# Attention ahead of two mixtures: row maxima scaled on ScalarE, the last batch turned in fp32 inside the loop, first weights of the second mixture split among the attention's units

## The chip, the cores and the metric

The kernel runs on one core of a Trainium2 chip. A core has TensorE (PE; its weight loads are shown as PEld), VectorE (DVE), ScalarE (ACT), GpSimd (POOL) and SyncE (SP), which here only issues DMAs. The metric is device microseconds of one execution. Lower is better.

## The reference

Three stages follow one another: a sparse attention, a mixture of eight experts in which each token goes to one expert, and a second mixture in which every token goes through all eight.

```python
# attention: B, H, S, D = 4, 8, 576, 64
scores = q @ k.T / 8                      # per batch and head
# heads 0-3: 0 <= i - j < 32;  heads 4-7: 0 <= i - j < 128 and (i - j) % 4 == 0
attn = softmax(where(mask, scores, -1e9));  x = attn @ v      # -> x [2304, 512]

# first mixture: N, D, E, F = 2304, 512, 8, 1024, capacity 288
logits = x @ w_gate
# pairs (token, expert) in falling order of logits; a token takes the first expert with room
out[mask_e] = relu(x[mask_e] @ w1[e]) @ w2[e]

# second mixture
P = exp(x @ w_gate - max); eight times: rows, then columns scaled to sums (Sinkhorn)
out = sum_e P[:, e] * (relu(x @ w1[e]) @ w2[e])
```

## The kernel before

The order of the instructions on each engine is written out by hand: the program emits them in the order in which each engine is to run them, and each engine and each DMA queue works through its own list in that order, waiting where an operand isn't ready.

**Attention** (`attention`, line 107). Queries go in 24 blocks of 96 (4 batches of 6). The dilated heads have their tokens reordered on the host so that both kinds of heads look at a band of 128 keys. A *unit* (`UNITS`, 25 of them, numbered 0 to 24) is one block of the plain heads (kind 0) with the next block of the dilated ones (kind 1); the first and the last unit are halves. The loop over `n` is a pipeline: step n takes the scores and row maxima of unit n, the transposes of unit n-1 and the products with v of unit n-2. Its order per step is: `scores(n)` on TensorE (line 167 adds the masks, line 174 is q times k); `row_max(n)` on VectorE (line 180 the maximum of 8 rows of 128, line 181 its product with -0.125, from a small tile `negc`); `p_trans(n-1)` on TensorE (line 197), copied to SBUF on VectorE (line 204); `exps(n)`, eight activations on ScalarE with the scaled maximum as bias (line 189); `pv(n-2)` on TensorE (line 215) with, from unit 13 on, products of one ready chunk of 128 tokens with the gate (`logits`, line 280), and on VectorE the reciprocal of the sums and the normalised block `xt` (lines 219 to 221) and the copy of the gate product (line 282); last `x_out(n-3)`, which splits `xt` into two fp16 halves `xo`: the high half copied by ScalarE (line 232), the low half by a subtraction on GpSimd (line 234; for the last two units on VectorE), and stores them to `xd` in HBM through SP's queue (line 237). `xo` has two buffers.

The gate needs x transposed. For batches 0 to 2 a transposing DMA brings chunks back from `xd` (line 262). Blocks of the last batch keep their `xo` in SBUF, and `x_turn` transposes its halves on TensorE (line 250, fp16, eight per unit) and copies them with ScalarE into `xl` (line 254). This is done for seven units behind the steps 24, 25, 26 and 27 (`TURN`). The last five chunks of gate products follow (line 280), and their copy ends the attention (line 335).

All q and k of batches 1 to 3 and v of batch 1 are sent for ahead of the loop (lines 121, 125).

**First mixture** (`Moe.stage1`, line 1146). `Router.phase(0)` finds the first expert and its tokens: VectorE compares all logits with thresholds (line 476), TensorE counts (line 480), VectorE picks a digit (lines 482 to 490), six times over. Between these steps `warm` runs filler products on TensorE (line 643), 5 or 1 at a time, and a generator `w0 = self.weights(("b", 0), ...)` loads six of eight pieces (128 x 1024, fp32, 512 KB) of the second mixture's first expert and splits them: high half on ScalarE (line 679), low half on VectorE (line 680). Then 16 filler products, and the first expert's own work: its weights are gathered by GpSimd (line 700) and split by the same two lines, its tokens gathered (line 709), transposed (line 744) and multiplied (lines 731, 768). The remaining two pieces of `("b", 0)` follow in its course. The other experts' routing is interleaved with the products from there on; the second mixture's first expert is computed block by block (lines 731 and 812), the other seven in `stage2`.

Of the kernel before, what the change touches and what calls it, by code (L numbers as in the profile page):

```python
# [23 lines left out]
QB = 96  # L24
# [59 lines left out]
TURN = {NU - 1: (NU - 7, NU - 6), NU: (NU - 5, NU - 4), NU + 2: (NU - 2, NU - 1)}  # L84
# [22 lines left out]
def attention(tc, q, k, v, masks, wg, ident, xd, L, zero):  # L107

    nc = tc.nc
    with ExitStack() as ctx:  # L110
# [8 lines left out]
        def load_qk(nm, b, kind):  # L119
            x = raw[nm, b, kind] = one.tile([128, 2, S], F32, name="raw%s%d%d" % (nm, kind, b))  # L120
            nc.sync.dma_start(x, src[nm][b, :, 2 * kind:2 * kind + 2])
# [13 lines left out]
        negc = one.tile([QB, 2, 4], F32)  # L135
        nc.gpsimd.memset(negc, -SC)
# [40 lines left out]
        def row_max(u):  # L177
            p, gs = SS[u], part(u, 4)
            nm = wk.tile([QB, 2, 4], F32, name="nm")
            nc.vector.tensor_reduce(nm[:, :, gs], p[:, :, gs], axis=AX.X, op=OP.max)  # L180
            nc.vector.tensor_mul(nm[:, :, gs], nm[:, :, gs], negc[:, :, gs])
            PP[u] = nm

        def exps(u):
            p, nm, gs = SS.pop(u), PP[u], part(u, 4)
            e = wk.tile([QB, 2, 4, 128], F32, name="e")
            for s in range(2):
                for g in range(gs.start, gs.stop):
                    nc.scalar.activation(e[:, s, g, :], p[:, s, g, :], AF.Exp, bias=nm[:, s, g:g + 1], scale=SC)
            PP[u] = e  # L190
# [15 lines left out]
        def pv(u, extra):  # L206
            t = PT.pop(u)
            tag, bufs = ("ps_v", 1) if u + 1 < NU else ("ps_s", 2)
            p = ps.tile([128, 2, 512], F32, name=tag, bufs=bufs)
            pp = p[:QB, :, :4 * (D + 1)].rearrange("p k (h d) -> p k h d", h=4)  # L210
            hs, ks = part(u, H), part(u, 2)
            for h in range(hs.start, hs.stop):
                o = pp[:, h // 4, h % 4, :]
                b, j = UNITS[u][h // 4]
                nc.tensor.matmul(o, t[:, h % 2, h // 2, :], VR[b, h // 4][:, j, h % 4, :], start=True, stop=True)  # L215
            fin = [logits(p[:, 0, 480 + E * n:480 + E * (n + 1)], c) for n, c in enumerate(extra)]
            rc = wk.tile([QB, 2, 4, 1], F32, name="rc")
            xt = wk.tile([QB, 2, 4, D], F32, name="xt")
            nc.vector.tensor_scalar(rc[:, ks], pp[:, ks, :, D:], 1e-9 / SX, None, op0=OP.add)
            nc.vector.reciprocal(rc[:, ks], rc[:, ks])  # L220
            nc.vector.tensor_mul(xt[:, ks], pp[:, ks, :, :D], rc[:, ks].to_broadcast([QB, ks.stop - ks.start, 4, D]))
            XT[u] = xt
            for f in fin:
                f()

        def x_out(u):
            xt, ks = XT.pop(u), part(u, 2)
            if u in XO:
                xo = XO[u]
            else:  # L230
                xo = wk.tile([QB, 2, 2, 4, D], F16, name="xo")
# [10 lines left out]
        def x_turn(*units):  # L242

            for u in units:
                p = ps.tile([128, 2, 512], F32, name="ps_s").bitcast(F16)[:, :, :4 * QB].rearrange(
                    "p k (c q) -> p k c q", c=4)
                ks = part(u, 2) if u > (B - 1) * NJ else slice(1, 2)
                for kind in range(ks.start, ks.stop):
                    for c in range(4):
                        nc.tensor.transpose(p[:, kind, c, :], XO[u][:, kind, c // 2, 2 * (c % 2):2 * (c % 2) + 2, :],  # L250
                                            idh)
                for kind in range(ks.start, ks.stop):
                    for o, n, tok, st in tokens_of(QB * UNITS[u][kind][1], QB, kind):
                        nc.scalar.activation(xl[kind][:, :, tok:tok + st * (n - 1) + 1:st], p[:, kind, :, o:o + n],
                                             AF.Copy)

        XB, XO = {}, {}
# [8 lines left out]
        def left(c, a, x):  # L266

            t0 = 128 * c - S * (B - 1)
            if x == 0:
                return XB[c][:, a, :]  # L270
            return xl[a // 4][:, a % 4, max(t0, 0):t0 + 128]

        def logits(p, c):
            cut = S * (B - 1) - 128 * c
            for x, rows in ((0, slice(0, min(cut, 128))), (1, slice(max(cut, 0), 128))):
                n = 0
                for kt in range(4 if rows.start < rows.stop else 0):
                    hi = kt if kt < 2 else kt + 2
                    for a, w in ((hi, wgh), (hi, wgl), (hi + 2, wgh)):
                        nc.tensor.matmul(p[rows], left(c, a, x), w[:, kt, :], start=(n == 0), stop=(n == 11))  # L280
                        n += 1
            return lambda: nc.vector.tensor_copy(L[:, c, :], p)
# [5 lines left out]
        for b in range(1, B if True else 2):  # L288
            for kind in (1, 0):
                for nm in "kq":  # L290
                    load_qk(nm, b, kind)
            if b == 1:
                for kind in (1, 0):
                    load_v(b, kind)
        nc.scalar.activation(wgh, wgf, AF.Copy, scale=SG)
        nc.vector.scalar_tensor_tensor(wgl, wgf, SG, wgh, op0=OP.mult, op1=OP.subtract)
        xl = [one.tile([128, 4, S], F16, name="xl%d" % kind) for kind in range(2)]
        for n in range(NJ + 1):
            XO[(B - 1) * NJ + n] = one.tile([QB, 2, 2, 4, D], F16, name="xo%d" % n)
        first = S * (B - 1) // 128  # L300
        for n in range(NU + 3):
# [5 lines left out]
            if n < NU:  # L307
                exps(n)
            if n in FILL:
                warm(FILL[n])  # L310
            if n == NU + 1:
                x_turn(NU - 3)
            if 2 <= n <= NU + 1:
                pv(n - 2, [loaded.pop(0)[1] for _ in range(1 if n < NU else 2) if loaded and loaded[0][0] <= n])
# [3 lines left out]
            if n >= 3:  # L318
                x_out(n - 3)
# [9 lines left out]
            x_turn(*TURN.get(n, ()))  # L329
        p = ps.tile([128, 2, 512], F32, name="ps_v", bufs=1)  # L330
        rest = [i for _, i in loaded] + list(range(first, NT))
# [61 lines left out]
class Router:  # L393
# [39 lines left out]
    def start(self, ctx):  # L433
        self.wk = ctx.enter_context(self.tc.tile_pool(name="r_wk", bufs=2))
# [169 lines left out]
class Moe:  # L604
    def __init__(self, ctx, tc, router, xd, ident, w1a, w2a, wg2, w1b, w2b, out, ps, zero):
        nc = self.nc = tc.nc
        self.tc, self.r, self.xd, self.out, self.ps = tc, router, xd, out, ps
# [3 lines left out]
        self.big, self.raw, self.sm = pool("m_big", 1), pool("m_raw", 4), pool("m_s", 1)  # L611
# [3 lines left out]
        self.acc = self.big.tile([128, NT, DM], F32, name="acc")  # L615
# [6 lines left out]
        self.W, self.balanced, self.scattered = {}, False, []  # L622
        self.wb = [[self.big.tile([128, 4, 7, 256], F16, name="w%d%s" % (n, c)) for c in "hl"] for n in (1, 2)]
# [11 lines left out]

    def psum(self):
        return self.ps.tile([128, 512], F32, name="mm", bufs=6)
# [7 lines left out]
    def weights(self, key, letter, fetch, some=slice(None)):  # L645
# [9 lines left out]
        todo = todo[some]  # L655
        live, tiles = [], {lay: t for (k, lay), t in self.W.items() if k == key}
# [13 lines left out]
        for n in range(len(todo)):  # L670
            (lay, k, per, m), r = live.pop(0)
            if lay not in tiles:
                if letter == "a":
                    tiles[lay] = [self.wp.tile([128, (KT, FT)[lay], m], F16, name="w%d%s" % (lay, c)) for c in "hl"]
                else:
                    tiles[lay] = self.wflat[lay]
                self.W[key, lay] = tiles[lay]
# [468 lines left out]
    def stage1(self, ctx):  # L1146

        pool = lambda n, b: ctx.enter_context(self.tc.tile_pool(name=n, bufs=b))
# [4 lines left out]
        self.wp = pool("m_w", 1)  # L1153
# [8 lines left out]
        for _ in w0:  # L1162
            pass
# [6 lines left out]
        def fetched(ph):  # L1170
            w = self.weights(("a", ph), "b", self.fetch_gather(ph))
# [5 lines left out]
        first = itertools.chain(fetched(0), self.weights(("b", 0), "a", self.fetch_static(0), slice(6, None)))  # L1177

        self.ready = self.direct(1)
        def main():  # L1180
# [10 lines left out]
            for ph in range(E):  # L1191
# [8 lines left out]
                for i, ns in enumerate(self.moe1(ph)):  # L1200
                    if ph + 1 == E and i in (16, 40, 44, 52, 56):
                        next(self.ready)
                    if ph == 0 and i % 6 == 1 and ws[0] is first:
                        pump(ph, FT + 4)
                        if ws[1] == FT + 4:
# [20 lines left out]
        self.warm(16)  # L1226
# [65 lines left out]
def tile_kernel(ctx, tc, q, k, v, wg, w1a, w2a, wg2, w1b, w2b, masks, ident, rtab, thr, out):  # L1292
    nc = tc.nc
    with tc.manual_schedule():
# [5 lines left out]
        attention(tc, q, k, v, masks, wg, ident, xd, L, router.zero)  # L1300
        ps = ctx.enter_context(tc.tile_pool(name="ps", bufs=2, space=bass.MemoryType.PSUM))
        router.ps = ps
        moe = Moe(ctx, tc, router, xd, ident, w1a, w2a, wg2, w1b, w2b, out, ps, router.zero)
        with ExitStack() as stage:
            moe.stage1(stage)
# [21 lines left out]
```

## Time and profile before

| | |
|---|---|
| three runs, us | 1835.52, 1838.80, 1842.16 (median 1838.80) |
| profiled execution, us | 1833.92 |
| its span, first to last instruction, us | 1832.1 |
| busy in the span | PE 96%, PEld 71%, DVE 75%, ACT 46%, POOL 12% |
| mean granted TensorE clock | 0.979 of full speed |

The profile is of one execution. The span leaves out 1.8 us around the instructions. Attention ends at 128.2 us, the first expert's routing at 161.8 us. Names like `xo` or `w0l` are the program's tiles; `out<-in` gives what an instruction writes and reads, with shapes as partitions x elements. In brackets stands how long the engine had been idle before the instruction and what ended that. Matmul ends are modelled, so a TensorE that looks busy may be waiting a little.

### The profile page before, as it was taken

The numbers are of one execution on the slowest core, as the hardware profiler recorded it, in microseconds if no ns is written. First come the engines' busy times: TensorE is split into PE (matmuls) and PEld (weight loads), VectorE is DVE, ScalarE is ACT, GpSimd is POOL, SyncE is SP. The second block draws the span as 40 slices with busy tenths as digits, with TensorE's granted clock in tenths as the row PEclk, the third lists the DMA queues.
The fourth block names the chain that finished last, engine by engine and source line by source line (L and its number), as shares of the span: only waits on it lengthen the run. The fifth ranks groups of instructions, "written<-read, shape, count | busy, mean of one in ns | idle before, by whom it ended". The sixth has DMA issues, their size and how long they took to land.

```text
span 1832.1 us, 35300 instructions
## 1 busy us (share of the span) xinstructions
PE 1752.7 (96%) x14518; PEld 1297.8 (71%) x14518; DVE 1371.9 (75%) x2625; ACT 839.1 (46%) x1502; POOL 227.4 (12%) x284
## 2 busy tenths in 40 slices
PE   8986899999999889999999999999999999999998
PEld 6873666666677647766777777777777777777776
DVE  5877776686744767877887888788878878887656
ACT  4662333333344344564444555444555444554333
POOL 1224222233221000000000000000000000000111
PEclk8988899999999999999999999999999999999999
DMA  8554323343242314433244432444352353433120
GB/s 304 148 138 138 110 83 95 109 119 104 88 142 83 122 47 156 147 131 146 112 167 164 184 125 105 171 156 152 136 195 93 127 213 140 163 122 141 55 96 35
DMA packets 106161, 241.19 MB, mean 132 GB/s; under 512 B 46704, under 2 KB 70512, under 8 KB 99088
## 3 DMA queue, kind: packets, MB, share of 16 engines
q1 hardware_dynamic: 84736, 151.34, 23.9%
q0 software_dynamic: 20592, 87.53, 13.4%
q8 instruction: 113, 1.85, 0.4%
q14 instruction: 48, 0.39, 0.1%
q10 hardware_dynamic: 672, 0.08, 0.0%
HBM read 173.83 MB, written 61.73 MB: 129 GB/s over the span
## 4 chain that ended last, share of the span: by engine, by line
PE 70%; DVE 11%; issue 10%; ACT 4%; DMA 3%; POOL 1%; SPq 0%; POOLq 0%; ACTq 0%; DVEq 0%
PE mm L995 26%; PE mm L1033 22%; PE mm L731 8%; PE mm L812 5%; PE mm L768 2%; PE ps_v L215 1%; PE r L480 1%; PE ps_p L197 1%; DVE hl L952 1%; PE ps_s L174 1%; POOL out_dram L1047 1%; DVE w1l L680 1%; DMA wgf<-in_wg_dram 1%; DMA rawk<-in_k_dram 1%; DVE G L552 1%
## 5 line engine op out<-in xcount | busy, mean ns | idle before, releaser
L995 PE MATMUL mm<-xb,w1h 128*128 128x384 f16 x2352 | 574.6, 327 | 5.3 <-DVE mm L966 4.9
L1033 PE MATMUL mm<-w2h,hh 128*128 128x256 f16 x1764 | 480.8, 273 | 8.5 <-DVE t L1059 4.4
L1033 PE MATMUL mm<-w2h,hl 128*128 128x256 f16 x1764 | 480.8, 273 | 0.0
L1033 PE MATMUL mm<-w2l,hh 128*128 128x256 f16 x1764 | 480.8, 273 | 0.0
L995 PE MATMUL mm<-xb,w1l 128*128 128x384 f16 x1176 | 383.9, 326 | 0.0
L1033 PEld LDWEIGHTS <-hh 128*128 128x128 f16 x3528 | 345.2, 98 | 52.6 <-issue 10.6
L995 PEld LDWEIGHTS <-w1h 128*128 128x128 f16 x2352 | 230.4, 98 | 159.5 <-issue 11.6
L1033 PEld LDWEIGHTS <-hl 128*128 128x128 f16 x1764 | 172.6, 98 | 20.0
L952 DVE TENSOR_TENSOR hl<-r,hh 128x1536 f16<-128x1536 f32 x84 | 147.5, 1756 | 41.2 <-ACT hh L951 41.2
L995 PEld LDWEIGHTS <-w1l 128*128 128x128 f16 x1176 | 115.2, 98 | 76.5 <-issue 0.7
L947 ACT ACTIVATE r<-mm 128x384 f32<-128x384 f32 x252 | 119.0, 481 | 98.3 <-PE mm L995 98.3
L951 ACT ACTIVATE hh<-r 128x1536 f16<-128x1536 f32 x84 | 124.6, 1483 | 46.4 <-DVE r L976 44.4
L913 POOL DMA_DIRECT2D ws<-raw x48 | 26.0, 541 | 941.1 <-ACT raw L864 673.6
L958 ACT ACTIVATE mm<-mm 128x384 f32<-128x384 f32 x84 | 40.3, 479 | 180.8 <-PE mm L995 180.8
L952 DVE TENSOR_TENSOR hl<-S,hh 128x1152 f16<-128x1152 f32 x84 | 113.6, 1352 | 0.0
L731 PE MATMUL mm<-xt,w1h 128*128 128x288 f16 x512 | 97.2, 289 | 1.4 <-ACT xt L745 1.4
L1043 DVE SCALAR_TENSOR_TENSOR acc<-t,P,acc 128x512 f32<-128x512 f32 x126 | 94.8, 752 | 4.5
L951 ACT ACTIVATE hh<-S 128x1152 f16<-128x1152 f32 x84 | 96.4, 1147 | 0.0
L864 ACT ACTIVATE raw<-raw 128x1024 f16<-128x1024 f32 x48 | 50.6, 1055 | 96.6 <-DVE raw L849 47.7
L734 ACT ACTIVATE w1h<-mm 128x288 f16<-128x288 f32 (+1 forms) x120 | 47.1, 397 | 102.6 <-PE mm L731 100.5
L735 DVE SCALAR_TENSOR_TENSOR w1l<-mm,w1h 128x288 f16<-128x288 f32 (+1 forms) x120 | 50.7, 435 | 55.1 <-ACT w1h L734 54.5
L731 PE MATMUL mm<-x2l,w0h 128*128 128x256 f16 x288 | 81.1, 282 | 6.8 <-DVE x2l L773 6.8
(258 smaller groups left out, 2972.1 us busy)
## 6 DMA issues: line engine op xcount, KB each, us to landing
xb<-xw SPq DMA_DIRECT2D x30, 1344.0 KB, 5.6
ws<-raw POOLq DMA_DIRECT2D x48, 448.0 KB, 2.7
ws<-r POOLq DMA_DIRECT2D x48, 448.0 KB, 3.0
raw<-in_w2b_dram SPq DMA_DIRECT2D x32, 512.0 KB, 9.4
raw<-in_w1b_dram SPq DMA_DIRECT2D x56, 256.0 KB, 6.3
w1h<-ws SPq DMA_DIRECT2D x6, 1792.0 KB, 7.5
w1l<-ws SPq DMA_DIRECT2D x6, 1792.0 KB
w2h<-ws SPq DMA_DIRECT2D x6, 1792.0 KB
```

Source lines behind the costliest of these rows:

```text
L731: nc.tensor.matmul(p, a[:, k, 128 * f:128 * (f + 1)], rhs(k, b), start=(k == 0 and i == 0), stop=(k == KT - 1 and i == 2))
L734: nc.scalar.activation(h[0][:, f, :n], p, AF.Relu)
L735: nc.vector.scalar_tensor_tensor(h[1][:, f, :n], p, 0.0, h[0][:, f, :n], op0=OP.max, op1=OP.subtract)
L812: nc.tensor.matmul(p, a[:, f, c], b[:, f, :], start=(f == 0 and n == 0), stop=(f == FT - 1 and n == 2))
L864: self.nc.scalar.activation(hi[:, k], x, AF.Copy, scale=sw)
L947: nc.scalar.activation(o, p, AF.Relu, scale=SH)
L951: yield nc.scalar.activation(hq[0][:, i, k], x, AF.Copy)
L952: yield V.tensor_sub(hq[1][:, i, k], x, hq[0][:, i, k])
L958: nc.scalar.activation(Q[i], P[i], AF.Copy)
L995: nc.tensor.matmul(p, w[u][:, 2 * j + i // 2, k, 128 * (i % 2):128 * (i % 2 + 1)], x[:, v, r, j], start=(q in (1, 5) and j == 0 and n == 0 ...
L1033: nc.tensor.matmul(p, h[u][:, i, a, 128 * t:128 * (t + 1)], w[v][:, i, b, :], start=(q in (1, 7) and i == 0 and j == 0), stop=(q in (2, 3) ...
L1043: V.scalar_tensor_tensor(self.acc[:, r, :], x, self.P[:, r, e:e + 1], self.acc[:, r, :], op0=OP.mult, op1=OP.add)
```

## The change

1. The product of the row maxima with -0.125 goes from VectorE to ScalarE (`row_max`). In step n the copy and subtraction of `x_out(n-3)` are emitted between the two halves of the exponentials, where they stood at the end of the step. `xo` gets four buffers, `xt` three.
2. The last batch is turned from `xt`, in fp32: `x_turn(u, p)` makes two transposes per kind into a free part of the tile of `pv`, then the high halves with ScalarE and the low halves with VectorE. Units 18 to 22 are turned in steps 21 to 25, ahead of that step's `pv`; units 23 and 24 behind the loop, ahead of their `x_out`. `xl` is laid out by half.
3. q and k of batches 2 and 3 are sent for in steps 6, 7, 12 and 13; only batch 1 is sent for ahead of the loop.
4. All eight pieces of the second mixture's first weights are loaded and split in the attention by a generator `first_weights`, called once in each step from 4 on: two steps with two loads each, then half a piece a step, with VectorE's half one step behind ScalarE's. The splits in `stage1` and in the first expert's products are gone.
5. For this, `Moe` is constructed ahead of the attention: its load of the identity (SP) and the cast of it (GpSimd) now stand ahead of the attention's loads. The pools of stage 1 lie on the other side of SBUF, and the large tiles are made behind the attention.
6. Filler products: 3 in place of 5 in the first routing, 6 in place of 16 behind it. More chunks of gate products are done in the steps, fewer behind them.

```diff
         def row_max(u):
...
-            nc.vector.tensor_mul(nm[:, :, gs], nm[:, :, gs], negc[:, :, gs])
+            nc.scalar.activation(nm[:, :, gs], nm[:, :, gs], AF.Copy, scale=-SC)
...
-        def pv(u, extra):
+        def pv(u, extra, turn=None):
...
+            if turn is not None:
+                x_turn(turn, p)
             for h in range(hs.start, hs.stop):
...
+            xo = wk.tile([QB, 2, 2, 4, D], F16, name="xo", bufs=4)
...
+        def x_turn(u, p):
+
+            p = p[:, :, 264:264 + 2 * QB].rearrange("p k (c q) -> p k c q", c=2)
+            ks = part(u, 2) if u > (B - 1) * NJ else slice(1, 2)
+            for kind in range(ks.start, ks.stop):
+                for c in range(2):
+                    nc.tensor.transpose(p[:, kind, c, :], XT[u][:, kind, 2 * c:2 * c + 2, :], idf[:QB, :QB])
+            parts = [(xl[kind][:, x, :, tok:tok + st * (n - 1) + 1:st], p[:, kind, :, o:o + n], x)
+                     for x in range(2) for kind in range(ks.start, ks.stop)
+                     for o, n, tok, st in tokens_of(QB * UNITS[u][kind][1], QB, kind)]
+            hi = [o for o, _, x in parts if x == 0]
+            for n, (o, i, x) in enumerate(parts):
+                if x == 0:
+                    nc.scalar.activation(o, i, AF.Copy)
+                else:
+                    nc.vector.tensor_sub(o, i, hi[n - len(hi)])
...
-        for n in range(NU + 3):
+        for n in range(NU + 2):
...
-            if n < NU:
-                exps(n)
+            ex = exps(n) if n < NU else iter(())
+            next(ex, None)
+            if 3 <= n <= NU:
+                x_out(n - 3)
+            for _ in ex:
+                pass
...
+            if n >= 2:
+                pv(n - 2, [loaded.pop(0)[1] for _ in range(1 if n < NU else 3) if loaded and loaded[0][0] <= n],
+                   n - 3 if NU - 4 <= n <= NU else None)
+            if 4 <= n:
+                next(side, None)
...
+            b, c = divmod(n - NJ, NJ)
+            if 0 <= b < B - 2 and c < 2:
+                for nm in "kq":
+                    load_qk(nm, b + 2, 1 - c)
...
+        x_turn(NU - 2, ps.tile([128, 2, 512], F32, name="ps_s"))
+        x_turn(NU - 1, ps.tile([128, 2, 512], F32, name="ps_p", bufs=1))
+        x_out(NU - 2)
+        x_out(NU - 1)
...
+    def first_weights(self, ctx):
...
+        for n, (lay, k, per, m) in enumerate(todo):
+            r = live.pop(0).rearrange("p k f -> p (k f)")
+            hi, lo = (t[:, k:k + per, :].rearrange("p k f -> p (k f)") for t in self.W[("b", 0), lay])
+            for c in (slice(0, 512), slice(512, 1024)):
+                nc.scalar.activation(hi[:, c], r[:, c], AF.Copy, scale=(SW1, SW2)[lay])
+                yield
+                nc.vector.scalar_tensor_tensor(lo[:, c], r[:, c], (SW1, SW2)[lay], hi[:, c], op0=OP.mult,
+                                               op1=OP.subtract)
+                if c.stop == 1024 and n + 4 < len(todo):
+                    load(n + 4)
...
-        w0 = self.weights(("b", 0), "a", self.fetch_static(0), slice(6))
-        next(w0)
         for i, need in enumerate(self.r.phase(0)):
-            self.warm(1 if need < 2000 else 5)
-            if i % 2 and i < 14:
-                next(w0, None)
+            self.warm(1 if need < 2000 else 3)
...
-        first = itertools.chain(fetched(0), self.weights(("b", 0), "a", self.fetch_static(0), slice(6, None)))
+        first = fetched(0)
...
-        self.warm(16)
+        self.warm(6)
...
-        attention(tc, q, k, v, masks, wg, ident, xd, L, router.zero)
...
+        moe = Moe(ctx, tc, router, xd, ident, w1a, w2a, wg2, w1b, w2b, out, router.zero)
         with ExitStack() as stage:
+            attention(tc, q, k, v, masks, wg, ident, xd, L, router.zero, moe.first_weights(stage))
+            moe.after_attention(ctx)
             moe.stage1(stage)
```

## Rows read from the trace of the kernel before

**Rows 1.** Chain of waits, two stretches: start us, us, what, instructions.

```profile
54.79 0.44 PE ps_s L167 x4
58.43 0.44 PE ps_s L167 x4
...
106.51 0.28 PE ps_v L280 x12
```

**Rows 2.** Timeline of VectorE (DVE), one unit: start us, duration us, instruction.

```profile
72.22 1.21 DVE L180 TENSOR_REDUCE nm<-ps_s 96x8 f32<-96x1024 f32 x1
73.46 0.83 DVE L181 TENSOR_TENSOR nm<-nm,negc 96x8 f32<-96x8 f32 x1
74.22 0.94 DVE L204 COPY pt<-ps_p 128x768 f32<-128x768 f32 x1
75.09 0.15 DVE L219 TENSOR_SCALAR rc<-ps_v 96x8 f32<-96x8 f32 x1
...
75.57 0.69 DVE L221 TENSOR_TENSOR xt<-ps_v,rc 96x512 f32<-96x512 f32 x1
...
76.25 1.21 DVE L180 TENSOR_REDUCE nm<-ps_s 96x8 f32<-96x1024 f32 x1
```

**Rows 3.** Timeline of GpSimd (POOL), the same unit.

```profile
73.12 1.15 POOL L234 TENSOR_TENSOR xo<-xt,xo 96x512 f16<-96x512 f32 x1 [2.88 <-ACT xo L232]
```

**Rows 4.** Timeline of ScalarE (ACT), the same unit.

```profile
72.39 0.65 ACT L232 ACTIVATE xo<-xt 96x512 f16<-96x512 f32 x1
74.41 2.15 ACT L189 ACTIVATE e<-ps_s,nm 96x128 f32<-96x128 f32 x8 [1.37 <-DVE nm L181]
```

**Rows 5.** Timeline of VectorE, the attention from unit 4 to its end.

```profile
27.13 1.22 DVE L180 TENSOR_REDUCE nm<-ps_s 96x8 f32<-96x1024 f32 x1 [0.32 <-PE ps_s L174]
...
53.95 0.16 DVE L181 TENSOR_TENSOR nm<-nm,negc 96x8 f32<-96x8 f32 x1
...
100.47 1.21 DVE L180 TENSOR_REDUCE nm<-ps_s 96x8 f32<-96x1024 f32 x1
...
112.57 0.68 DVE L180 TENSOR_REDUCE nm<-ps_s 96x4 f32<-96x512 f32 x1
...
128.00 0.20 DVE L335 COPY L<-ps_v 128x40 f32<-128x40 f32 x1 [3.30 <-PE ps_v L280]
```

**Rows 6.** Timeline of ScalarE, the first 42 us.

```profile
14.96 0.23 ACT L295 ACTIVATE wgh<-wgf 128x32 f16<-128x32 f32 x1 [11.98 <-DMA wgf<-in_wg_dram]
...
39.47 0.63 ACT L232 ACTIVATE xo<-xt 96x512 f16<-96x512 f32 x1 [4.62 <-DMA xd<-xo]
```

**Rows 7.** Stretch, its us, busy time by engine, then PEclk, DMA share, GB/s.

```profile
36.00:50.00 14.00, 11.63 (x85) 10.05 (x84) 7.38 (x13) 6.35 (x21) 3.46 (x3) 0.64 0.26 83
```

**Rows 8.** Line 254, 125 to 127 us: duration ns min/median/max, starts, form.

```profile
L254 ACT ACTIVATE xl<-ps_s x3: 491/585/1018, 125.1 to 126.3; 128x384 f16<-128x384 f16 x3
```

**Rows 9.** Timeline of TensorE (PE) at the start, first product.

```profile
12.13 0.38 PE L167 MATMUL ps_s<-mk,idb 96*96 96x256 bf16 x2 [4.60 <-DMA mk<-in_masks_dram]
```

**Rows 10.** Timeline of GpSimd at the start, the load of the masks.

```profile
2.64 0.55 POOL L148 DMA_DIRECT2D mk<-in_masks_dram  x1
```

**Rows 11.** Timeline of VectorE at the start, first use of the router's table.

```profile
7.02 0.23 DVE L425 CAST tri<-rtab 128x128 f16<-128x128 f32 x1 [5.61 <-DMA rtab<-in_rtab_dram]
```

**Rows 12.** Timeline of VectorE, routing of the first expert and after it.

```profile
132.39 0.27 DVE L482 TENSOR_SCALAR ok<-r,rem 8x64 f16<-8x64 f32 x1 [0.77 <-PE r L480]
132.94 0.23 DVE L488 TENSOR_SCALAR pen<-r 128x64 f32<-128x64 f32 x1 [0.27 <-PE r L485]
...
139.03 0.24 DVE L482 TENSOR_SCALAR ok<-r,rem 8x32 f16<-8x32 f32 x1 [0.47 <-PE r L480]
...
140.33 0.17 DVE L488 TENSOR_SCALAR pen<-r 128x32 f32<-128x32 f32 x1
...
176.27 1.23 DVE L680 SCALAR_TENSOR_TENSOR w2l<-raw,w2h 128x1024 f16<-128x1024 f32 x1 [2.73 <-ACT w2h L679]
```

**Rows 13.** Line 680 alone in a stretch: us, DVE busy (count), PEclk, DMA.

```profile
128.20:162.00 33.80, 7.26 (x6) 0.80 0.40 126
```

More of the change, by code (lines that the diff above doesn't have):

```diff
@@ L104, in lay_v, with attention @@
     return out
-def attention(tc, q, k, v, masks, wg, ident, xd, L, zero):
+def attention(tc, q, k, v, masks, wg, ident, xd, L, zero, side):
     nc = tc.nc
@@ L226, in x_out @@
         def x_out(u):
[L227 to L231, printed above, removed]
+            xt, ks = XT[u], part(u, 2)
+            xo = wk.tile([QB, 2, 2, 4, D], F16, name="xo", bufs=4)
             nc.scalar.activation(xo[:, ks, 0], xt[:, ks], AF.Copy)
@@ L240, in x_out @@
                         xo[p0:p0 + n, kind].rearrange("q a h d -> q (a h d)"))
[L242 to L257, printed above, removed]
+        def x_turn(u, p):
[13 more added lines that the diff above has]
+                    nc.vector.tensor_sub(o, i, hi[n - len(hi)])
+        XB = {}
         def x_load(c, c1):
@@ L328, in attention @@
                 x_load(first, first + 1)
-            x_turn(*TURN.get(n, ()))
+            if n == NU:
+                loaded += [(n, i) for i in (first, first + 1)]
+        x_turn(NU - 2, ps.tile([128, 2, 512], F32, name="ps_s"))
+        x_turn(NU - 1, ps.tile([128, 2, 512], F32, name="ps_p", bufs=1))
+        x_out(NU - 2)
+        x_out(NU - 1)
         p = ps.tile([128, 2, 512], F32, name="ps_v", bufs=1)
-        rest = [i for _, i in loaded] + list(range(first, NT))
+        rest = [i for _, i in loaded] + list(range(first + 2, NT))
         o = p[:, 0, :E * len(rest)].rearrange("p (n e) -> p n e", e=E)
@@ L604, with __init__ @@
 class Moe:
-    def __init__(self, ctx, tc, router, xd, ident, w1a, w2a, wg2, w1b, w2b, out, ps, zero):
+    def __init__(self, ctx, tc, router, xd, ident, w1a, w2a, wg2, w1b, w2b, out, zero):
         nc = self.nc = tc.nc
-        self.tc, self.r, self.xd, self.out, self.ps = tc, router, xd, out, ps
+        self.tc, self.r, self.xd, self.out = tc, router, xd, out
         self.w = {"a": (w1a, w2a), "b": (w1b, w2b)}
@@ L643, in warm, with weights @@
             self.nc.tensor.matmul(p, self.zero[:, :128], self.zero, start=True, stop=True)
-    def weights(self, key, letter, fetch, some=slice(None)):
+    def weights(self, key, fetch):
         nc = self.nc
@@ L654, in weights @@
                 todo.append((lay, k, per, m))
-        todo = todo[some]
-        live, tiles = [], {lay: t for (k, lay), t in self.W.items() if k == key}
+        live, tiles = [], {}
         def load(it):
@@ L672, in weights @@
             if lay not in tiles:
[L673 to L677, printed above, removed]
+                self.W[key, lay] = tiles[lay] = self.wflat[lay]
             hi, lo = (t[:, k:k + per, :] for t in tiles[lay])
```

92 lines of the change are left out of this document (46 added, 46 removed).

## Prediction

> **What bounds the kernel now.** I read the chain of waits first, then the timelines of the engines, unit by unit. The change touches only the attention (to 128.2 us) and the start of the first mixture, so the question is what sets the end there. In the early units the chain is TensorE without a gap: one unit takes 58.43 - 54.79 = 3.64 us [rows 1]. From about 58 us a unit takes 76.25 - 72.22 = 4.03 us, with gate products or without, and VectorE has no gap in it [rows 2]: the maximum 1.24 us to the next start, the multiplication with the negative scale 0.76, the copy of the turned exponentials 0.87, and reciprocal, product and gate copy 1.16. The multiplication has 8 elements a row and lasts 0.83 us where GpSimd's subtraction runs beside it, but 0.16 us alone [rows 2, 5]; it ends at 74.29, with GpSimd's instruction, at 73.12 + 1.15 = 74.27 [rows 3]. It waits for GpSimd, and the exponentials start 0.12 us behind it [rows 4]. One stall stands out: at 39.47 ScalarE had waited 4.62 us for the store of an earlier xo [rows 6], and TensorE's granted clock averages 0.64 around it [rows 7]. Behind the attention, the first expert's routing is a chain through VectorE, and six weight splits of line 680 (7.26 us) stand in it [rows 13].
>
> **The change part by part**, from the profiled execution (1833.92 us, span 1832.1; the median of the runs, 1838.8, lies 4.9 above it).
>
> *Start.* The mixture's constructor now runs first, so GpSimd casts the identity, and waits for its load, ahead of the load of the masks. The masks went out at 2.64 and the first product waited for them until 12.13 [rows 9, 10]. The cost is nothing if the identity lands at once, and 7.02 - 2.64 = 4.4 us at most if it is as late as the router's table [rows 11]. It is the first and a small load; I take 0.6.
>
> *Units 4 to 20.* From unit 4's maximum to unit 21's there are 100.47 - 27.13 = 73.3 us [rows 5], the stall included. The stall goes: only batch 1 is loaded ahead, and xo has four buffers. In its place each unit from 7 on carries half a split, 512 elements a row on VectorE. The nearest row with 512 elements is the product xt, 0.69 us, which the next instruction follows after 0.61 [rows 2]. So VectorE needs 1.24 + 0.87 + 1.16 + 0.60 = 3.87 us a unit: the half split takes back nearly all that the multiplication gave. Three units at 3.64 and fourteen at 3.87 are 65.1 us.
>
> What else these units get is covered: ScalarE has 0.23 + 2.15 + 0.65 and half a weight copy of some 0.55, 3.6 of 3.87 us; the copy of xo between the exponentials lets them end 0.12 + 0.23 + 2.15 + 0.55 = 3.05 behind the maximum, no later than today's 3.13 (74.41 + 2.15 against 72.22 + 1.21 [rows 2, 4]), so TensorE's transposes come no later. SP's queue gets eight loads of 512 KB, in units 4 and 5 and then one in two units, and batches 2 and 3 in the loop; stores of xo queue behind them, but each now has four units, 15 us. Without that cover the 4.62 us would be back.
>
> The half split reads two tensors of SBUF, as the multiplication did, and GpSimd's subtraction is still there. Which is first? From the maximum's end ScalarE needs 0.12 to start, 0.23 for the scaling (nearest row 0.23 [rows 6]), 1.0 for four exponentials (half of 2.15 [rows 4]) and 0.65 for the copy of xo, and GpSimd follows 0.08 behind (73.12 against 72.39 + 0.65) [rows 3, 4]: 2.1 us. VectorE comes to the split after 0.03 + 0.87 + 1.16 = 2.06 us. That is a tie, with VectorE ahead by 0.05. In a unit with gate products TensorE is 0.28 us later [rows 1], VectorE waits for it, GpSimd is first, and the split waits to 2.1 + 1.15 = 3.25: 1.2 us lost. In the unit after, TensorE has caught up and the tie is back. Units 13 to 16, 19 and 20 have gate products, so I count 13, 15, 19 and the first, 7: four times 1.2, 4.8 us. The bounds are 0 and 14 times (16.8). Sum 69.9, 3.4 less than before.
>
> The Trainium skill (SBUF — State Buffer, Who interferes with whom) says that a VectorE instruction with two SBUF inputs and a GpSimd instruction that reads SBUF exclude each other, and whichever starts first keeps the ports for its whole length. The 0.16 and 0.83 us above agree with it. By that rule alone, were GpSimd first in all units, the 65.1 would be 81.9.
>
> *Units 21 to 24* now turn a finished unit each, ahead of their own products. The halves are in VectorE's order ahead of the reciprocals: high half on ScalarE, behind all exponentials, then low half on VectorE. From the maximum's end: 0.12 + 0.23, exponentials 2.15, copy 0.55, 3.05 us. Then the high copies. A copy of 384 elements took 0.49 us contiguous and 1.02 with tokens four apart [rows 8]; half the size I estimate at 0.33 and 0.58. They end at 3.6 to 3.95, the last subtraction 0.4 later, then 1.16, in units 21 and 22 the half split 0.6, and the next maximum 1.24 (0.69 for unit 24's half): 7.0, 7.35 and 6.1, together 20.4 us. Before, the same way is 112.57 + 0.68 - 100.47 - 1.21 = 11.6 [rows 5]. So 8.8 us more: VectorE stands about 2.4 us in each unit, waiting for ScalarE. TensorE's clock may fall in these gaps as it did around 39 us [rows 7]; its 3.64 + 0.28 us of work a unit [rows 1] would be 6.1 at a clock of 0.64 and still fit into 7.
>
> *From unit 24's maximum to the end:* 128.20 - 113.25 = 14.95 us before [rows 5]. After, by the same pieces: ScalarE has two pairs of exponentials, a copy of xo and two high copies to 2.75, VectorE the low halves to 3.15 and the product xt of unit 22 to 4.3. Then the turn of 22: copy of xo 0.65, three high copies to 6.1, low halves to 6.5; TensorE's products of unit 23 and two chunks of gate products end at about 7.0, its xt at 8.3. Unit 24's products and three chunks end at 8.8, its xt at 9.8; the turns of 23 and 24 come straight from fp32, with no copy and subtraction of xo ahead of them, high halves to 10.5, low to 11.0. Four chunks of gate products are 4 x 0.28, waits and the last copy 0.7: 12.8. So 2.15 less; nothing, if the clock is at its lower level all the way.
>
> *Behind the attention.* Six splits leave the first routing. A search step without one goes from 132.39 to 132.94 before its penalty, one with it from 139.03 to 140.33 [rows 12]: 0.75 each, 4.5 us (bounds 0 and 7.26). Two more leave the first expert's products, where TensorE mostly covers them: 0.7 (0 to 2.4). The same expert's VectorE waits 2.73 us for gathered weights at 176.27 [rows 12]; the two loads of w2b that went out then are gone: 0.9 (0 to 2.7). The shorter filler runs (16 to 6, 5 to 3) I take at nothing, since these gathered weights come no sooner for it. Together 6.1.
>
> *Sum:* 0.6 - 3.4 + 8.8 - 2.15 - 6.1 = -2.3 us. On the median, 1836.5.
>
> **The rivals.**
> *The tie goes to VectorE always.* For it: the scaling may last longer than its row, as an instruction that the next one depends on, and GpSimd's start need not be its first read. Against: the margin in gate units is 0.2 us on the wrong side. The 4.8 us go, and if the gathers come 1 us sooner too, -8: 1831.
> *The tie goes to GpSimd always (the other side).* Place: line 680's successor in units 7 to 20, price 1.2 us each; it decides as soon as the split comes more than 0.05 us later than I count, say by slower pieces on VectorE. Ten more units pay, 12 us: -2.3 + 12 = +9.7, 1848.5. Against: every piece of VectorE's sum is a start-to-start distance, so little can be missing.
> *Late masks and a cold clock.* The identity's load as late as its bound (3.8 more than I take) and the end without its 2.15: +3.7, 1842.5. For it: the masks themselves took 12.13 - 2.64 = 9.5 us [rows 9, 10]; against: 64 KB at the head of a queue.
> *The turns cost nothing,* because VectorE had room there: -2.3 - 8.8 = -11, 1828. Against: in-order VectorE has the subtractions ahead of the reciprocals, and nothing else to do.
>
> **How the numbers follow.** A measurement tells some 0.3%, 5.5 us, from no change. Forecast (a few lost ties) 0.40; VectorE always 0.26; GpSimd always 0.14; late masks and clock 0.10; free turns 0.10. The forecast's own spread of some 4 us gives faster 0.08, same 0.30, slower 0.02; VectorE's case faster 0.21, same 0.05; GpSimd's slower 0.13, same 0.01; masks same 0.06, slower 0.04; free turns faster 0.10. Sums: faster 0.39, same 0.42, slower 0.19. The range leaves out the outer half of the free turns and of GpSimd's case: 1828 to 1847.
>
> **What would show it.** Right: no wait of ScalarE for a store near 39 us; units 8 to 12 of about 3.8 us with GpSimd's subtraction stretched or begun behind the half split; half splits of 1.2 us or more in units 13, 15, 19; units 21 to 23 of about 7 us, VectorE idle for ScalarE ahead of its subtractions; the first routing about 4.5 us shorter. Wrong: half splits that all last 0.7 or all 1.8 us; turn units near 4 us; a first product later than 13 us; or any move past 230 us, where nothing is changed.

## Result and profile after

The changed kernel takes 1857.41 us (median of 5 runs, 1853.84 to 1859.94), the kernel before beside it 1842.16 (1835.52 to 1843.53): ratio 1.0094, 95% interval 1.0081 to 1.0107, some 17 us slower (the two medians differ by 15.3). The forecast was 1836.5, the range 1828 to 1847. The profiled execution of after took 1859.94 us (span 1858.1, clock 0.969), that of before 1833.92 (0.979).

VectorE's timeline of the changed kernel, the answers to [rows 5]: the maxima of units 4, 21, 22, 23 and 24.

```profile
28.25 1.22 DVE L176 TENSOR_REDUCE nm<-ps_s 96x8 f32<-96x1024 f32 x1 [0.45 <-PE ps_s L170]
...
96.95 1.21 DVE L176 TENSOR_REDUCE nm<-ps_s 96x8 f32<-96x1024 f32 x1
...
108.29 1.22 DVE L176 TENSOR_REDUCE nm<-ps_s 96x8 f32<-96x1024 f32 x1 [1.03 <-PE ps_s L170]
...
120.14 1.22 DVE L176 TENSOR_REDUCE nm<-ps_s 96x8 f32<-96x1024 f32 x1 [1.03 <-PE ps_s L170]
...
130.71 0.69 DVE L176 TENSOR_REDUCE nm<-ps_s 96x4 f32<-96x512 f32 x1 [0.35 <-PE ps_s L170]
```

Units 4 to 21 take 68.70 us (before 73.34), units 21 to 24 33.76 (12.10), and the attention's last copy ends at 152.21 (128.20). What follows is told by VectorE's instruction that writes an expert's token index (`idx`) at the end of its search; first the changed kernel, then the one before (the times behind the comma are the first and the last start).

```profile
L572 DVE SCALAR_TENSOR_TENSOR idx<-s x8: 158/158/159, 180.6 to 524.8; 96x3 int32<-96x3 f32 x8
```

```profile
L572 DVE SCALAR_TENSOR_TENSOR idx<-s x8: 157/158/159, 161.6 to 501.9; 96x3 int32<-96x3 f32 x8
```

The first search got shorter, from 33.4 us behind that copy to 28.4. At the first index the changed kernel is 19.0 us late: +1.1 at unit 4, -4.6, +21.7, +5.9 (from the end of unit 24's maximum to the last copy, 20.81 for 14.95), -5.0. The profiled executions differ by 26.0 us; the other 7.0 lie behind this index. They need not come from the change: with the changed kernel's code from there on, run e1 below took 1668.1 us for that stretch, the changed kernel 1677.5, the kernel before 1670.5.

One unit with a turn in the changed kernel, all engines: ScalarE's exponentials and high halves, VectorE's low halves, TensorE's PV (the products with v), then its scores.

```profile
111.32 1.13 ACT L186 ACTIVATE e<-ps_s,nm 96x128 f32<-96x128 f32 x4
...
112.32 0.83 ACT L251 ACTIVATE xl<-ps_v 128x192 f16<-128x192 f32 x3
...
113.18 0.85 DVE L253 TENSOR_TENSOR xl<-ps_v,xl 128x192 f16<-128x192 f32 x3 [2.47 <-ACT xl L251]
...
114.08 2.83 PE L214 MATMUL ps_v<-rawv,pt 128*96 128x65 f32 x16 [3.74 <-DVE xl L253]
...
118.07 2.03 PE L170 MATMUL ps_s<-rawk,rawq 64*96 64x128 f32 x16
```

TensorE's work from PV to the scores does not overlap the chain from the maximum to the halves: the halves end at 114.03, PV starts 0.05 us behind them, and the next maximum (120.14) waits for the scores that end at 120.10. From maximum to halves it is 5.74 us, and TensorE's own 6.02 come on top. TensorE is also at half speed. Stretches of the changed kernel (columns as in [rows 7]), then of the kernel before:

```profile
28.00:97.00 69.00, 67.92 (x834) 60.05 (x830) 63.48 (x106) 57.12 (x188) 27.10 (x18) 1.00 0.84 259
97.00:130.00 33.00, 19.50 (x154) 17.36 (x156) 12.78 (x26) 10.90 (x37) 3.45 (x3) 0.65 0.24 57
130.00:152.00 22.00, 16.55 (x194) 14.96 (x191) 9.21 (x29) 5.94 (x17) 2.30 (x2) 0.50 0.10 25
```

```profile
97.00:130.00 33.00, 29.09 (x432) 24.95 (x431) 22.74 (x54) 21.55 (x59) 8.37 (x8) 0.88 0.45 103
```

The clock is 1.00 up to unit 21, then averages 0.65, and is 0.50 (the lower level, 1.2 of 2.4 GHz) to the attention's end.

### The profile page after: what moved, and what is told of

The parts are those of the page before. It is cut to its first block, busy times and chain, and to the rows that moved or that the text cites. A ratio compares the mean times of both kernels' runs of the same rounds, so it can differ in the third digit from the quotient of the medians.

```text
span 1858.1 us, 35250 instructions
## 1 busy us (share of the span) xinstructions
PE 1759.2 (95%) x14470; PEld 1305.4 (70%) x14470; DVE 1367.9 (74%) x2623; ACT 840.0 (45%) x1535; POOL 235.6 (13%) x283
## 4 chain that ended last, share of the span: by engine, by line
PE 71%; DVE 11%; issue 11%; ACT 4%; DMA 1%; POOL 1%; SPq 0%; POOLq 0%; DVEq 0%; ACTq 0%
PE mm L1029 25%; PE mm L1067 22%; PE mm L765 9%; PE mm L846 5%; PE ps_v L214 2%; PE mm L802 2%; DVE hl L986 1%; PE ps_s L170 1%; PE r L480 1%; DVE w1l L714 1%; PE ps_p L194 1%; POOL out_dram L1081 1%; DVE G L476 1%; DVE r L901 1%; ACT w1h L713 1%
## 5 line engine op out<-in xcount | busy, mean ns | idle before, releaser
L768 ACT ACTIVATE w1h<-mm 128x288 f16<-128x288 f32 (+1 forms) x120 | 46.7, 396 | 108.6 <-PE mm L765 92.7
```

The lines of the kernel that those rows point to most:

```text
L768: nc.scalar.activation(h[0][:, f, :n], p, AF.Relu)
```

## Experiments

My theory: in the five units with a turn, PV stands behind the turn in the same tile (`ps_v`) of two banks of PSUM, the memory that takes TensorE's results; two engines' accesses to these banks are kept apart, so TensorE waits for VectorE's low halves, and these for ScalarE; the gaps take TensorE's clock, which makes the rest of the chain longer. Rivals: VectorE's order alone, the clock alone, the other parts of the change. Each run's time is the median of 5 to 12 executions. The kernel before had medians from 1833 to 1842 us beside the different groups of runs, so the ratios are compared. In the table the times of units (u4-21 is from unit 4's maximum to unit 21's) and of the first index come from each run's profiled execution.

| run | median us | ratio to before, 95% | u4-21 | u21-24 | u24 to last copy | first index |
|---|---|---|---|---|---|---|
| before | 1833 to 1842 | 1 | 73.34 | 12.10 | 14.95 | 161.6 |
| changed | 1857.41 | 1.0094 (1.0081-1.0107) | 68.70 | 33.76 | 20.81 | 180.6 |
| e1_other_banks | 1834.48 | 1.0004 (0.9995-1.0013) | 68.73 | 22.61 | 17.71 | 164.9 |
| e2_turn_behind | 1834.25 | 0.9999 (0.9985-1.0013) | 68.73 | 21.19 | 19.86 | 166.7 |
| e3_filled | 1844.04 | 1.0056 (1.0043-1.0069) | 68.42 | 29.43 | 18.33 | 172.3 |
| e4_old_turn | 1825.70 | 0.9949 (0.9936-0.9962) | 72.05 | 19.03 | 15.48 | 162.3 |
| e5_logits_later | 1825.62 | 0.9955 (0.9943-0.9968) | 67.43 | 12.12 | 18.36 | 155.7 |
| e6_split_first | 1817.60 | 0.9915 (0.9902-0.9928) | 64.26 | 11.50 | 16.58 | 148.8 |
| e7_banks_behind | 1830.63 | 0.9987 (0.9979-0.9996) | 69.65 | 18.14 | 17.71 | 162.2 |
| e8_banks_all | 1826.15 | 0.9964 (0.9952-0.9976) | 64.30 | 17.98 | 14.76 | 155.0 |
| e9_turn_alone | 1866.20 | 1.0147 (1.0129-1.0165) | 71.51 | 33.00 | 20.42 | 188.4 |
| e10_changed_split_first | 1856.32 | 1.0095 (1.0079-1.0112) | 68.20 | 34.27 | 20.81 | 180.4 |
| e11_max_on_vector | 1827.33 | 0.9941 (0.9923-0.9959) | 66.07 | 11.37 | 15.69 | 149.8 |
| e12_two_buffers | 1828.32 | 0.9953 (0.9936-0.9971) | 68.61 | 11.49 | 15.70 | 152.5 |
| e13_old_split_first | 1825.72 | 0.9951 (0.9934-0.9968) | 67.55 | 11.50 | 15.30 | 151.8 |
| e14_changed_both | 1850.71 | 1.0078 (1.0065-1.0091) | 64.29 | 34.27 | 21.20 | 175.8 |

**The turn in other banks (e1).**

```diff
-                x_turn(turn, p)
+                x_turn(turn, ps.tile([128, 2, 512], F32, name="ps_p", bufs=1))
```

> The five turns that stand ahead of PV go to the PSUM banks of the P transposes (free once P is evacuated) in place of PV's own; place in the program and order on every engine stay. Theory of the shared banks (TensorE's PV waits for VectorE's low halves because turn and PV are in one pair of banks, and the gap halves the clock): the waits of 5.58 and 3.74 us in front of PV's 16 products fall under 1.5 us, units 21 to 24 take 20 to 26 us in place of 33.8, and the whole is 10 to 18 us shorter than the changed kernel. Rival of VectorE's order (the low halves stand ahead of PV's reciprocals on VectorE whatever bank they read): PV's products come early but the unit does not get shorter, 30 us or more for units 21 to 24, under 6 us gained. Rival of the next transposes: they now wait for the low halves in PV's stead, and nothing is gained.

**The turn behind PV (e2),** in PV's banks: the call of `x_turn(turn, p)` moves from ahead of PV's products to the end of `pv`.

> The five turns stay in PV's banks but stand behind PV's products, the reciprocals and the products on VectorE. Theory of the shared banks: PV no longer waits for a turn of its own unit; the next unit's PV waits for the low halves, which end a unit's time earlier than before, so units 21 to 24 take 18 to 24 us in place of 33.8 and the whole is 10 to 18 us shorter than the changed kernel. Rival of VectorE's order: the low halves still stand ahead of the next maximum, so about as long as with the other banks. If the sharing is nothing and the turn's own work is too long for these units: 30 us or more, under 4 us gained.

Both bring back all that the change had lost, 0.9% or some 17 us. In e1 only the tile changed, and no engine's order: so the shared tile holds PV. Another tile means other banks here, so e1 does not tell the tile from its banks. TensorE now stands at the turn itself (e1, its timeline), for the evacuation of P, the copy of the turned exponentials to SBUF:

```profile
106.24 0.55 PE L244 MATMUL ps_p<-idf,xt 96*128 96x96 f32 x4 [1.17 <-DVE pt L201]
...
113.62 0.55 PE L244 MATMUL ps_p<-idf,xt 96*128 96x96 f32 x4 [2.77 <-DVE pt L201]
```

The units are still nearly twice as long as before the change (22.61 and 21.19 for 12.10).

**Fillers against the cold clock (e3).**

```diff
                 x_turn(turn, p)
+                f = ps.tile([128, 2, 512], F32, name="ps_s")
+                for _ in range(12):
+                    nc.tensor.matmul(f[:, 0, :], zero[:, :128], zero, start=True, stop=True)
```

> The changed kernel with 12 filler products of 512 columns in a free bank between a turn's transposes and PV in the five units. Rival of the clock alone (the units are long because TensorE fell to half its clock, and the waits are only a consequence): the clock of 100 to 150 us rises from 0.57 towards 0.9, PV's 16 products go from 2.8 back to 1.4 us and 8 to 12 us come back in units 21 to 24. Theory of the shared banks: VectorE's and ScalarE's chain is as long as before and the fillers (2.6 us at the high level, 5.1 at the low one) only lie in the gap; the units get shorter by what TensorE's own work loses, some 1.5 to 3 us each, 5 to 10 us in all, and stay over 7.5 us each.

TensorE's timeline and one stretch of e3:

```profile
100.74 1.90 PE L217 MATMUL ps_v<-rawv,pt 128*96 128x65 f32 x16 [3.00 <-DVE xl L256]
...
121.11 1.81 PE L217 MATMUL ps_v<-rawv,pt 128*96 128x65 f32 x16 [2.34 <-DVE xl L256]
```

```profile
100.00:150.00 50.00, 42.70 (x418) 30.35 (x419) 24.69 (x67) 13.83 (x45) 4.61 (x4) 0.79 0.24 51
```

The clock of 100 to 150 us rises from 0.57 to 0.79 and PV's products fall from 2.83 to 1.9 us, but PV still waits for the halves and a unit takes 9.8 us. 0.38%, some 7 us, come back: the clock is a part of the loss. The wait is another, as the theory had it; how the rest divides is open, as the clock was not brought back whole.

**The turn alone, and all but the turn (e9, e4).** e4 is the changed kernel with the turn, `xl`, `left` and the seven kept `xo` of the kernel before; e9 is the kernel before with the new `x_turn`, its places, its logits and three `xt`.

> The changed kernel with the turn of the kernel before: fp16 halves kept in seven buffers of their own, turned in the score banks two units at a time, copied by ScalarE alone. All other parts of the change stay. Theory: the rest of the change gains 4.6 us in units 4 to 21 and 4.9 in the first search and loses 1.1 at the start, so this kernel is 6 to 12 us faster than the kernel before, and 22 to 30 faster than the changed one. Rival that another part costs (the buffers, the order of loads, what comes behind attention): no faster than the kernel before.

> The kernel before with the new turn alone (fp32 products turned in PV's banks ahead of PV, high halves by ScalarE, low halves by VectorE); maxima, buffers, loads and the weights' splits stay as before. Taken from the runs so far (changed kernel +17 us on the kernel before, with the old turn -8): the new turn alone costs 18 to 28 us, PV waits 3 us or more for the low halves in units 21 to 23, and TensorE's clock is at half for most of 100 to 130 us. Rival: the turn costs only together with the other parts (ScalarE's extra work, the loads, the splits), under 12 us here.

The new turn alone costs 1.47%, some 27 us, and everything else gains 0.51%, some 9; the sum, 18, is the change. TensorE in e9:

```profile
105.28 2.82 PE L216 MATMUL ps_v<-rawv,pt 128*96 128x65 f32 x16 [4.66 <-DVE xl L255]
...
116.65 2.82 PE L216 MATMUL ps_v<-rawv,pt 128*96 128x65 f32 x16 [3.25 <-DVE xl L255]
```

In e4 units 21 to 24 were long as well, 19.03 us, in the profiled execution (1832.46 us, the longest of its five; the others are 1823 to 1826). TensorE's timeline tells why, and two stretches of it show the clock:

```profile
86.62 1.50 PE L213 MATMUL ps_v<-rawv,pt 128*96 128x65 f32 x16
89.75 0.18 PE L278 MATMUL ps_v<-wgh,xT 128*128 128x8 f16 x1 [1.63 <-DMA xT<-xd]
...
100.16 2.71 PE L213 MATMUL ps_v<-rawv,pt 128*96 128x65 f32 x16
```

```profile
92.00:96.00 4.00, 4.00 (x37) 4.00 (x36) 2.19 (x3) 2.70 (x10) 0.77 (x1) 0.50 0.53 122
112.00:116.00 4.00, 4.00 (x33) 3.72 (x32) 2.40 (x3) 1.45 (x6) 0.00 (x0) 0.56 0.89 126
```

It stood 1.63 us for a transposed load of x, and from 91.7 to 115 us, at a clock of 0.50, its work took about twice as long.

**Later logits, the split ahead of the reciprocals (e5, e6, e10, e13, e14).** In e5 and e6 on e4's kernel:

```diff
-                    loaded += [(n + 3, i) for i in range(c0, c1)]
+                    loaded += [(n + 3 + (n < 20), i) for i in range(c0, c1)]
```

and in e6 `next(side, None)`, the half split, moves from behind `pv` to ahead of it.

> The changed kernel with the turn of before (as in the run before), and the logits of the first two batches' loads due one unit later. There TensorE waited 1.63 us for a transposed load at 88.1, its clock fell to half at 91.7 and stayed there to 115, and units 21 to 24 took 19.0 us where the kernel before takes 12.1. Theory of the clock (one wait for a load that comes late costs four units): the wait is gone, the clock stays at 1.00 up to 112, units 20 to 24 take 16 to 18 us in place of 25.9 and the whole is 7 to 11 us shorter than with the old turn alone, 15 to 20 under the kernel before. Rival: the clock falls at another gap all the same (VectorE's collisions with GpSimd), under 3 us gained.

> As the run with the later logits, and the half split of the weights ahead of PV's reciprocals on VectorE in place of behind them. Theory of the collisions: the split (0.68 us alone, 1.70 beside GpSimd's subtraction) no longer meets GpSimd, the three long ones go, 1 to 4 us gained. Rival: the reciprocals come 0.7 us later in each unit and PV's banks with them, TensorE waits, 0 to 5 us lost and perhaps the clock with them.

e5's expectation failed: the wait is gone and units 21 to 24 take 12.12 us, but the median is that of e4, whose other executions were as short already. e6 gains 8 us on e5, twice the most that I had expected, and is the fastest kernel, 15.8 us under the one before. Its maxima of units 4, 21 and 24, and the stretch of the loop:

```profile
27.54 1.22 DVE L177 TENSOR_REDUCE nm<-ps_s 96x8 f32<-96x1024 f32 x1 [0.45 <-PE ps_s L171]
...
91.80 1.22 DVE L177 TENSOR_REDUCE nm<-ps_s 96x8 f32<-96x1024 f32 x1 [0.15 <-PE ps_s L171]
...
103.30 0.68 DVE L177 TENSOR_REDUCE nm<-ps_s 96x4 f32<-96x512 f32 x1
```

```profile
28.00:97.00 69.00, 69.00 (x875) 62.57 (x874) 64.51 (x113) 59.95 (x196) 20.83 (x18) 1.00 0.84 262
```

TensorE is busy throughout. Then each edit's share, with the old turn (e13: e6 without the later logits) and in the changed kernel (e10: the split first; e14: both):

> The changed kernel with the turn of before and the split first, the logits due as in the change. Theory of the late load (a faster loop reaches the logits before the transposed load has landed, as at 88.9 us with the split first alone; TensorE stands 1.3 us or more and its clock may fall): most of what the two edits give together (-15.8 us on the kernel before) is lost, 6 to 11 us under the kernel before. Rival: the split's place is worth 6 us or more by itself, 14 us or more under it.

> The changed kernel with one edit: the half split of the weights ahead of PV's reciprocals on VectorE. Theory: the three long splits go (some 1 us each) and nothing else in units 4 to 20; the turn's waits stay: 2 to 5 us shorter than the changed kernel, still 12 us or more slower than the kernel before. Rival: what the split's place gave with the old turn (8 us) comes from the turn units and their clock, then 6 to 10 us here as well.

> The changed kernel, turn in PV's banks ahead of PV, with both the split first and the later logits. Theory: units 4 to 21 take 64 to 65.5 us in place of 68.7, the turn units keep their waits: 3 to 6 us under the changed kernel, 11 to 14 over the kernel before. Rival: the turn units lose what the loop gains (PV waits for the same halves, the clock is down anyway), within 2 us of the changed kernel.

e10 gives nothing, where I had expected 2 to 5 us, e13 nothing over e4, and both edits together 6 to 7 us over either alone with the old turn. In the changed kernel both give some 3 us (e14), within the overlap of the two intervals. TensorE of e10, then of e13:

```profile
88.88 0.18 PE L272 MATMUL ps_v<-wgh,xT 128*128 128x8 f16 x1 [1.31 <-DMA xT<-xd]
```

```profile
88.01 0.18 PE L278 MATMUL ps_v<-wgh,xT 128*128 128x8 f16 x1 [1.22 <-DMA xT<-xd]
```

Without the long splits the loop reaches the logits before the load has landed: unit 19 took 6.18 us in e10 and 6.00 in e13, 3.69 in e6. What the split gave, the load took: units 4 to 21 take 68.20 us in e10 and 64.29 in e14.

**The new turn without either wait (e7, e8).** e7 has the turn behind PV and in `ps_p`; e8 adds the two edits.

> The changed kernel's fp32 turn in the banks of the P transposes and behind PV. In those banks but ahead of PV TensorE waited 2.58, 1.17 and 2.77 us for the evacuation of P; in PV's banks but behind it 2.12, 1.40 and 1.73 us for the logits' copy; here it waits for neither. Theory of the waits: units 21 to 24 take 14 to 18 us (22.6 and 21.2 there), the clock of 100 to 115 stays above 0.9 and the whole is 4 to 9 us shorter than in those two runs. Rival of the fp32 turn itself (ScalarE's and VectorE's halves are too long for the unit): 20 us or more for units 21 to 24, under 2 us gained.

> As the run with the turn behind PV in the banks of the P transposes, with the later logits and the split ahead of the reciprocals. If the two small edits act by themselves: 1 to 5 us shorter than without them. If the fp32 turn has no cost of its own, this kernel equals the one with the old turn and the same two edits within 2 us; if its halves cost time, it is 3 to 8 us slower than that one.

e7 gains only some 2.5 us on e1 and e2, where I had expected 4 to 9: the wait moved to the next unit's transposes, which need the same banks (e7, TensorE):

```profile
102.54 0.88 PE L194 MATMUL ps_p<-idf,e 96*128 96x96 f32 x8 [1.30 <-DVE xl L253]
...
108.79 1.47 PE L194 MATMUL ps_p<-idf,e 96*128 96x96 f32 x8 [1.70 <-DVE xl L253]
```

e8 is 8.5 us slower than e6, from which it differs by the turn alone; 6.5 of it lie in units 21 to 24 (17.98 for 11.50). So the new turn, handed from TensorE to ScalarE to VectorE, has a price in any banks that were tried. How much of it is waits and how much the clock was not separated.

**Two terms of the sum (e11, e12),** undone in e6: the maxima scaled by VectorE's multiplication with `negc`, and `bufs=2` for `xo`.

> The fastest kernel so far (old turn, later logits, split first) with the maxima scaled on VectorE as before the change. Theory of the two engines' shared access (VectorE's 0.83 us beside GpSimd, 0.16 without): VectorE has the half split and the scaling in a unit whose other work takes 3.7 us, 0.8 us more in each of units 4 to 21, so 8 to 16 us longer. Rival: TensorE's products set the unit, under 3 us longer.

> The fastest kernel so far with two buffers for xo in place of four. Theory: ScalarE waits again for the stores of two units before it, where their queue is late, some 4 to 8 us longer, at the places where the kernel before stood (around 40 us). Rival: the order of the loads alone removed the stall, within 2 us.

e11 costs 0.26%, some 5 us (the two intervals just overlap), less than expected. VectorE from 28 to 97 us, by line (count, busy us, mean ns):

```profile
L180 DVE TENSOR_TENSOR nm<-nm,negc 96x8 f32<-96x8 f32 x18 | 2.9, 162 | 0.6
```

The multiplication lasts 0.16 us each time: in e6's order GpSimd's subtraction does not lie beside it, and of the 0.83 us [rows 2] nothing was left to save. Units 4 to 21 take 1.8 us more, but at the first index the profiled execution is only 1.0 us behind e6's (149.8 for 148.8): where the 5 us are is open. e12 costs 0.38%, some 7 us; ScalarE waits for stores again, though not around 40 us but here:

```profile
52.76 0.63 ACT L230 ACTIVATE xo<-xt 96x512 f16<-96x512 f32 x1 [0.74 <-DMA xd<-xo]
56.90 0.63 ACT L230 ACTIVATE xo<-xt 96x512 f16<-96x512 f32 x1 [0.71 <-DMA xd<-xo]
73.58 0.63 ACT L230 ACTIVATE xo<-xt 96x512 f16<-96x512 f32 x1 [1.46 <-DMA xd<-xo]
```

## Why the prediction was wrong

**The step that failed** is "Units 21 to 24". It had VectorE stand "about 2.4 us in each unit, waiting for ScalarE", and TensorE's work at the low clock "still fit into 7". VectorE's wait was right (2.47 us for the high halves). But I let TensorE work beside that chain. PV shares its tile with the turn, so TensorE's PV, gate products and scores come behind the low halves and ahead of the next maximum: 5.74 + 6.02 us are added where I took the longer of the two. 20.4 us became 33.2, counted as there from one maximum's end to the next (33.76 from start to start). That both are in `ps_v` stands in the code, and no wait in the trace of before showed what it costs. By e1 against the changed kernel some 16 us hung on the choice of the tile.

The Trainium skill (PSUM — Partial Sum Buffer, PSUM bank collisions raise a hardware error) says that two engines must not touch one bank in the same partitions at once, whatever the columns, and that semaphores have to keep them apart. The trace shows such a wait: PV starts 0.05 us behind the last low half though its columns are others. But in the first of the five turns the wait goes beyond that rule. Only the dilated half of unit 18 is turned there, in the second half of the tile (`ks` is 1 alone, two transposes), and in the code's order PV's products for heads 0 to 3 come first and go to the first half; they waited as well:

```profile
96.33 0.33 PE L244 MATMUL ps_v<-idf,xt 96*128 96x96 f32 x2
102.24 2.82 PE L214 MATMUL ps_v<-rawv,pt 128*96 128x65 f32 x16 [5.58 <-DVE xl L253]
```

So the wait here seems to go by the program's tile. That is read from the trace and the code: no run gave the turn a tile of its own in PV's banks, or left the wait out.

**The clock.** "TensorE's clock may fall in these gaps" was right, its price not: the loss is not hidden where TensorE is in the chain. At the upper level TensorE's 6.02 us would be about 3 (an estimate, half of it); e3 got a part of that back.

**From unit 24's maximum to the end:** 12.8 us forecast, 20.81 measured, in part the same mistake. TensorE, three times in the changed kernel:

```profile
134.95 2.82 PE L214 MATMUL ps_v<-rawv,pt 128*96 128x65 f32 x16 [2.18 <-DVE xl L253]
139.14 0.88 PE L244 MATMUL ps_v<-idf,xt 96*128 96x96 f32 x4 [0.73 <-DVE xt L220]
141.81 2.83 PE L214 MATMUL ps_v<-rawv,pt 128*96 128x65 f32 x16 [1.79 <-DVE xl L253]
```

I had written "nothing, if the clock is at its lower level all the way"; it was, and it came out 5.9 worse. Two of these three waits are for the low halves; e1, without them, took 17.71. How the rest divides between the clock and the order of the turns is open.

Both steps together miss by 12.8 + 8.0 = 20.8 us, and the median lies 20.9 above the forecast. That the two agree so well is partly luck. The steps are read from profiled executions that differ by 26.0 us where -2.3 was forecast, a miss of 28.3; the rest of it are the smaller terms up to the first index (+0.5, -1.2 and -0.5) and the 7.0 us behind it, where -1.6 was forecast.

**The start:** 0.6 forecast, 1.1 measured in that execution; the first product came at 12.15, so the masks were not late. Unit 4's maximum lies between 26.9 and 28.4 us in the runs, so the difference is no more than executions differ.

**Units 4 to 20:** 69.9 forecast, 68.70 measured, for the reasons given. The stall is gone, and three half splits ran beside GpSimd, in units 14, 16 and 20 (four were forecast, in 7, 13, 15 and 19). GpSimd's and VectorE's rows of the last:

```profile
95.20 1.28 POOL L230 TENSOR_TENSOR xo<-xt,xo 96x512 f16<-96x512 f32 x1 [2.11 <-ACT xo L228]
...
95.34 1.68 DVE L669 SCALAR_TENSOR_TENSOR w1l<-raw,w1h 128x512 f16<-128x512 f32 x1
```

The others take 0.68 us. GpSimd began 0.14 us ahead and the split lasted 1.0 longer (I had 1.2). e6 shows what I did not see, that the order which avoids this was one line away, and that a late load stands behind it.

**Behind the attention:** 4.5 us forecast for the search, 5.0 measured; in e9, which keeps the splits there, it took 34.5 us, in all other experiments 28.2 to 29.0. Whether the 0.7 and 0.9 us for the first expert came is not shown. Its first product comes 9.8 us behind the first index, 12.2 before, with six fillers in place of 16, a term that I took at nothing. But the second index comes 50.9 us behind the first, 50.5 before, and 46.7 in e1, whose code is the changed kernel's there: executions differ by more than these terms. So they do for the move past 230 us that I had named as a sign of being wrong: from the last index to the end it is 1333.3 us after, 1330.2 before, and 1330.7 in e3, whose code there is the changed kernel's too.

**The rivals.** None had the mechanism. The one on the slow side, GpSimd first in every unit, gave 1848.5 for another reason; the free turns were as wrong as could be.

## What to carry to other kernels

Before work of another engine is put into a PSUM tile that TensorE is about to use, count the tile as a lock: what stands ahead is added to TensorE's time, not laid beside it (whether a tile of one's own in a shared bank would do was not tried). Where a chain crosses three engines in one unit, price TensorE's own part at the lower clock too. An edit that shortens a loop can show nothing until the transfer that then comes late is moved with it: try the two together.

## What was unexpected in the hardware

One wait of 1.63 us for a load was followed by half clock from 91.7 to 115 us in e4, while TensorE was busy all the time (4.00 of each 4 us from 92 to 116); in e13, after the unit with the wait of 1.22 us, one unit took 4.94 us and the next 3.95 again. And the time behind the attention is not fixed: with the same code from the first index to the end, the profiled executions of the changed kernel and of e1 took 1677.5 and 1668.1 us, so part of e6's lead, 12.8 us at the first index and 16.3 at the end, may be of that kind.
